# Retention and token-mixing kernel: full-height chunk tiles, decay on v and on the result, a new order of the steps

## The chip, the cores and the metric

The kernel runs on one core of one Trainium2 chip. The metric is the device time of one execution in microseconds (us). A profile covers the span from the first to the last instruction; the time is 1.7 to 2.0 us longer than the span (3.4 and 3.6 in two runs of experiment 11). Each run comes with the TensorE clock that was granted on average, and with a state: "slow" is put on a run that is over 1.5% above the fastest run of the same kernel.

In the profile PE is the matmul engine, PEld its weight loads, DVE the vector engine, ACT the scalar engine, POOL the GpSimd engine and SP the engine that issues most DMAs.

## The reference, cut to what matters

```python
# q, k, v: (4 batches, 8 heads, 768 tokens, 64); gamma[h] = 1 - 2**(-5-h)
for t in range(S):                         # retention, per batch and head
    state = gamma * state + outer(k[t], v[t])
    y[t]  = q[t] @ state / 8
x = y laid out as (batch, token, 512)      # then the token mixer
wq, wk = x @ w_q, x @ w_k                  # 512 x 64 each
mixed  = (wq @ wk.T / 8) @ x               # per batch; done as wq @ (wk.T @ x)
out    = relu(mixed) @ w_out               # 512 x 512
```

## The kernel before

The sequence is cut into 12 pairs of two 128-token chunks, three pairs per batch. The decay is folded into the operands: gamma^t times q and gamma^-t times k make the recurrence a plain masked product within a chunk (`sc`, `eat`, `ia`) plus a running state (`state`, `inter`). A load puts two consecutive tokens on each partition, so a chunk fills only 64 partitions, and everything whose contraction runs over tokens or over one head's 64 channels uses 64-row matmuls.

```python
def decay(e, p, name, table, half):              # q and k: cast and decay in one, 128 x 1024
    ENGINES[e].tensor_tensor(out=st[name + "s"]..., in0=st[name + "_st"]..., in1=table..., op=ALU.mult)
def cv(e, b, p):                                 # v: a plain cast, 128 x 1024
    copy(e, st["vs"]..., st["v_st"]...)
...
def sc(e, b, p, half):                           # scores: 16 matmuls of 64 x 64
    for hi in range(2):
        for j in range(2):
            for x in range(2):
                for c in range(2):
                    nc.tensor.matmul(out=ps[rows(c), x, hi, j, :], lhsT=st["kT"][rows(x), hp, j, c, :],
                                     rhs=st["qT"][rows(x), hp, c, :], ...)
...
def X(e, b, p):                                  # inter and state streams taken two and two in turn
    together(inter(p, 0), state(p, 1))
...
def ia(e, b, p, half):                           # masked scores times v: 16 matmuls, 64 rows each
    ... nc.tensor.matmul(out=st["y_ps"][:, c, x, hp, :], lhsT=st["at", half][rows(c), x, hi, j, :],
                         rhs=st["vs"][rows(c), hp, j, x, :], ...)
def ex(e, b, p):                                 # result out of PSUM: a plain cast
    copy(e, st["x"]..., st["y_ps"]...)
```

The order of all steps, with the engine of each evacuation and the PSUM bank, is a fixed list of tokens. `ex.3:A` is step `ex` of pair 3 on ACT (V is DVE, P is POOL), `sc.3.1@4` is the second half of the scores of pair 3 into bank 4. `trk` and `trq` transpose k and q, `xt` the result, `pj` is the projection by w_out, `eo` its evacuation, `fill` are matmuls on zeros that keep the array busy.

## Time and profile before

| | before |
|---|---|
| median of 3 runs | 106.53 us (106.33 to 107.72) |
| profiled run | 107.5 us, span 105.8, clock 0.96, state slow |
| last matmul group starts / last store lands | 94.09 / 105.8 us |
| loads | 20.19 MB, DMA full until about 70 us |

The prediction shows the slices, the stretches and the costly groups. Three lines of the page that it doesn't show matter later: the busy sums, ACT's slices (tenths of busy time, 40 slices of 2.65 us), and the queue that brings the instructions themselves (packets, MB, share of the DMA engines' time).

```profile
PE 90.7 (86%) x2040; PEld 63.3 (60%) x2040; DVE 77.0 (73%) x108; ACT 54.6 (52%) x87; POOL 46.1 (44%) x41
ACT  5103344713257546297679498648457184564010
...
q8 instruction: 16, 0.26, 1.0%
```

PE runs 2040 matmuls, and ACT and POOL are half idle: there is room there to pay for less PE work. The instruction queue moved 16 packets of 16 KB.

### The profile page before, as it was taken

Reading aid. Unit: us, or ns where it says so; the run is one execution under the profiler, and the core shown is the slowest. Engines: PE = TensorE matmul, PEld = TensorE weight load, DVE = VectorE, ACT = ScalarE, POOL = GpSimd, SP = SyncE. Lnnn points to the kernel's source line nnn. Section 1 sums busy time; section 2 is a strip of 40 time slices with the busy share of each in tenths; the row PEclk is TensorE's granted clock in tenths of the full one; section 3 lists DMA queues with packets and bytes.
Section 4 is the critical chain, followed back from the end, with each engine's and each line's share of the span. In section 5 each row is a group of like instructions: output and inputs, shape, how many; then the busy total and the mean of one; then the engine's idle time right before and its main releaser. Section 6 shows DMA issues by size and latency. Waiting matters only on the chain. (4 is left out here: it accounts for less than half of the span.)

```text
span 105.8 us, 4560 instructions
## 1 busy us (share of the span) xinstructions
PE 90.7 (86%) x2040; PEld 63.3 (60%) x2040; DVE 77.0 (73%) x108; ACT 54.6 (52%) x87; POOL 46.1 (44%) x41
## 2 busy tenths in 40 slices
PE   5997986849999996998999699689999999999800
PEld 2354664638888873595777566369668676554300
DVE  2097978836669899997589996999787976319800
ACT  5103344713257546297679498648457184564010
POOL 6620762985999315692977094990000000000000
PEclk9999999975599999999999999999999999999996
DMA  1999998999999999999999999999133060661993
GB/s 31 311 347 336 346 344 274 345 344 266 323 305 333 299 306 339 315 313 309 257 282 324 270 265 331 327 344 295 34 96 109 0 184 20 198 178 27 336 346 114
DMA packets 52324, 26.77 MB, mean 253 GB/s; under 512 B 848, under 2 KB 52304, under 8 KB 52304
## 3 DMA queue, kind: packets, MB, share of 16 engines
q1 hardware_dynamic: 51776, 26.22, 83.8%
q8 instruction: 16, 0.26, 1.0%
q10 hardware_dynamic: 528, 0.26, 0.8%
q14 instruction: 4, 0.03, 0.1%
HBM read 20.19 MB, written 6.29 MB: 250 GB/s over the span
## 5 line engine op out<-in xcount | busy, mean ns | idle before, releaser
L345 DVE TENSOR_TENSOR at_sb<-banks,cmask 128x1024 bf16<-128x1024 f32 x24 | 28.9, 1220 | 7.6 <-PE banks L333 7.4
L263 POOL TENSOR_TENSOR ks<-k_st,fk 128x1024 bf16<-128x1024 f32 (+1 forms) x10 | 18.4, 1841 | 13.7 <-DMA k_st<-in_k_dram 6.5
L569 PE MATMUL banks<-wout_sb,relu 128*128 128x512 bf16 x96 | 23.0, 379 | 1.2 <-DVE wout_sb L127 1.0
L263 POOL TENSOR_TENSOR qs<-q_st,fq 128x1024 bf16<-128x1024 f32 x9 | 17.6, 1956 | 6.9 <-DMA q_st<-in_q_dram 5.6
L126 ACT CAST x_nat<-banks 128x1024 bf16<-128x1024 f32 x11 | 11.1, 1012 | 8.2 <-PE banks L399 7.4
L569 PEld LDWEIGHTS <-relu 128*128 128x128 bf16 x96 | 8.6, 97 | 10.3 <-issue 1.7
L126 ACT COPY o_st<-banks 128x512 f32<-128x512 f32 x15 | 8.6, 589 | 9.0 <-PE banks L569 8.9
L333 PE MATMUL banks<-qT,kT 64*64 64x128 bf16 x384 | 10.6, 226 | 3.0 <-issue 1.6
L251 PE MATMUL banks<-warm 128*128 128x512 bf16 x32 | 10.2, 454 | 2.0 <-DVE warm L190 1.2
L333 PEld LDWEIGHTS <-kT 64*64 64x64 bf16 x384 | 7.0, 109 | 5.7 <-issue 2.4
L399 PE MATMUL banks<-s_sb,qT 64*64 64x64 bf16 x320 | 10.1, 200 | 0.1
L399 PE MATMUL banks<-vs,ks 64*64 64x64 bf16 x320 | 8.8, 194 | 1.3 <-issue 1.1
L436 PE MATMUL banks<-vs,at_sb 64*128 64x64 bf16 x384 | 9.3, 195 | 0.2 <-DVE at_sb L345 0.2
L562 ACT ACTIVATE relu<-banks 128x1024 bf16<-128x1024 f32 x7 | 7.2, 1027 | 4.0 <-PE banks L547 3.7
L477 PE MATMUL banks<-wqk_w,xT 128*128 128x128 bf16 x96 | 8.2, 234 | 1.1 <-issue 1.0
L126 ACT COPY kT<-banks 128x1024 bf16<-128x1024 bf16 x7 | 7.1, 1013 | 3.5 <-PE banks L297 3.2
L399 PEld LDWEIGHTS <-qT 64*64 64x64 bf16 x320 | 7.6, 112 | 2.0 <-issue 0.8
L463 PE MATMUL banks<-identity,x_nat 128*128 128x128 bf16 x96 | 8.1, 227 | 0.6 <-issue 0.5
L436 PEld LDWEIGHTS <-at_sb 64*128 64x128 bf16 x384 | 7.4, 97 | 2.0 <-issue 0.8
L477 PEld LDWEIGHTS <-xT 128*128 128x128 bf16 x96 | 6.5, 105 | 2.8 <-issue 1.3
L399 PEld LDWEIGHTS <-ks 64*64 64x64 bf16 x320 | 6.9, 109 | 1.8 <-issue 1.6
L126 ACT CAST s_sb<-banks 128x256 bf16<-128x256 f32 x14 | 5.3, 378 | 5.0 <-PE banks L399 5.0
(55 smaller groups left out, 135.5 us busy)
## 6 DMA issues: line engine op xcount, KB each, us to landing
q_st<-in_q_dram SPq DMA_DIRECT2D x12, 512.0 KB, 6.3
v_st<-in_v_dram SPq DMA_DIRECT2D x12, 512.0 KB, 6.7
k_st<-in_k_dram SPq DMA_DIRECT2D x11, 512.0 KB, 6.8
out_dram<-o_st SPq DMA_DIRECT2D x11, 512.0 KB, 4.3
wout_stage<-in_moe_w_out_dram SPq DMA_DIRECT2D x1, 1024.0 KB, 8.6
out_dram<-o_st SPq DMA_DIRECT2D x2, 256.0 KB, 3.3
k_st<-in_k_dram ACTq DMA_DIRECT2D x1, 256.0 KB, 4.3
k_st<-in_k_dram SPq DMA_DIRECT2D x1, 256.0 KB, 3.9
```

The lines of the kernel that those rows point to most:

```text
L126: return nc.scalar.copy(out=out, in_=in_)
L251: nc.tensor.matmul(out=bank32(b), lhsT=warm[:, 0:128], rhs=warm, start=True, stop=True)
L263: ENGINES[e].tensor_tensor(out=st[name + "s"][:, :, :, xs].rearrange("p hp j x d -> p x (hp j) d"), in0=st[name + "_st"][:, xs].rearrange( ...
L333: nc.tensor.matmul(out=ps[rows(c), x, hi, j, :], lhsT=st["kT"][rows(x), hp, j, c, :], rhs=st["qT"][rows(x), hp, c, :], start=(hi == 0 and ...
L345: ENGINES[e].tensor_tensor(out=st["at", half].rearrange("p x hi j t -> p (x hi) (j t)"), in0=st["at_ps", half].rearrange("p (xhi jt) -> p ...
L399: out.append(nc.tensor.matmul(skip_group_check=True, **mm))
L436: nc.tensor.matmul(out=st["y_ps"][:, c, x, hp, :], lhsT=st["at", half][rows(c), x, hi, j, :], rhs=st["vs"][rows(c), hp, j, x, :], start=fi ...
L463: nc.tensor.transpose(ps[:, a, c, :], st["x"][:, c, a, :], identity)
L477: nc.tensor.matmul(out=ps[:, c, :], lhsT=st["xT"][:, a, c, :], rhs=wqk_sb[:, a, :], start=(c == 0 and a == 0), stop=(a == NDM - 1), skip_g ...
L562: nc.scalar.activation(out=dst, in_=st["mx_ps"], func=ACT.Relu)
L569: nc.tensor.matmul(out=bank32(b), lhsT=st["relu"][:, a, j, :], rhs=wout_sb[:, a, :], start=(a == 0), stop=(a == NDM - 1),)
```

## The change

The intent: full-height (128-row) matmuls where there were pairs of half-height ones. For that the casts of k and v write the two tokens of a partition onto two different partitions, so that a chunk covers all 128. The scores and `inter` still contract over one head's 64 channels; they now fill all 128 output columns instead. Such a cast needs two instructions of 64 partitions x 512 elements per chunk. The decay moves from q and k to v (gamma^-t, table `fv`) and to the result (gamma^t, table `fy`), which makes q's cast a plain copy and the evacuation `ex` a multiply. Casts and evacuations are dealt out anew among the engines, and the whole order is new.

```diff
+    def ck(e, b, p, c):
+        for j in range(2):
+            copy(e, st["ks"][rows(j), c].rearrange("p hp x d -> p x hp d"),
+                    st["k_st"][rows(c), :, :, j])
+    def cv(e, b, p, c):
+        for j in range(2):
+            ENGINES[e].tensor_tensor(out=st["vs"][rows(j), c]..., in0=st["v_st"][rows(c), :, :, j],
+                                     in1=fv[rows(c), p % NP, :, j]..., op=ALU.mult)
...
     def sc(e, b, p, half):
-            for j in range(2):
+            for c in range(2):
                 for x in range(2):
-                    for c in range(2):
-                        nc.tensor.matmul(out=ps[rows(c), x, hi, j, :], lhsT=st["kT"][rows(x), hp, j, c, :], ...
+                    nc.tensor.matmul(out=ps[:, x, hi, c, :], lhsT=st["kT"][rows(x), hp, c, :], ...
...
-                        lhsT=st["ks"][rows(c), hp, j, x, :],     # state: 64 rows
-                        rhs=st["vs"][rows(c), hp, j, x, :],
+                    lhsT=st["ks"][:, c, hp, x, :],               # state: 128 rows
+                    rhs=st["vs"][:, c, hp, x, :],
...
-                            lhsT=st["at", half][rows(c), x, hi, j, :],   # ia
-                            rhs=st["vs"][rows(c), hp, j, x, :],
+                        lhsT=st["at", half][:, x, hi, c, :],
+                        rhs=st["vs"][:, c, hp, x, :],
...
     def ex(e, b, p):
-        copy(e, st["x"]..., st["y_ps"]...)
+        nc.vector.tensor_tensor(out=st["x"]..., in0=st["y_ps"]..., in1=fy[...].to_broadcast([128, 2 * H, D]), op=ALU.mult)
```

Left out here: the tables; the smaller mask; the two interleaved streams with their manual dependency, which become separate steps `st` and `in`; w_q and w_k loaded later and in 256-byte rows, w_out in four DMAs; the new order (W cast on ACT, WO on POOL, five more fills).

## The prediction

> **What bounds the kernel now.** I read first the slices of the page (busy tenths of each engine in 40 slices of 2.65 us, then the granted clock, the DMA share and the GB/s).
>
> ```profile
> PE   5997986849999996998999699689999999999800
> DVE  2097978836669899997589996999787976319800
> POOL 6620762985999315692977094990000000000000
> PEclk9999999975599999999999999999999999999996
> DMA  1999998999999999999999999999133060661993
> ```
>
> Two phases show. Until slice 28 (about 72 us) the DMA is full: it brings in q, k and v, and POOL, which casts them, ends with it. After that the DMA is mostly idle and PE alone is full until 100 us. The table of stretches (busy us of each engine in each stretch, clock, DMA share, GB/s) puts numbers to this:
>
> ```profile
> 6.00:30.00 24.00, 20.03 (x481) 15.30 (x481) 17.54 (x24) 9.12 (x11) 14.17 (x10) 0.86 1.08 322
> 30.00:70.00 40.00, 36.03 (x1023) 26.91 (x1015) 35.16 (x43) 26.47 (x43) 26.60 (x16) 1.00 1.05 307
> 70.00:90.00 20.00, 19.66 (x480) 14.48 (x470) 16.67 (x24) 12.22 (x23) 1.22 (x2) 1.00 0.41 122
> 90.00:100.30 10.30, 10.23 (x69) 4.86 (x68) 6.17 (x9) 4.58 (x8) 0.00 (x0) 1.00 0.61 183
> ```
>
> The columns are PE, weight load, DVE, ACT, POOL. From 30 to 70 us PE (90%) and DVE (88%) share the bound with loads at 307 GB/s; from 70 to 100.3 PE is 98% busy and nothing else is. The chain that ended last agrees: from 69.1 us on it is PE work with hardly a wait, and it ends so:
>
> ```profile
> 93.24 0.84 PE banks L547 x12
> 94.09 6.16 PE banks L569 x28
> 100.25 0.02 issue
> 100.27 0.58 ACT o_st L126
> ```
>
> Then 5 us of store follow to 105.8. POOL's timeline has the last v cast where the loads end, with no wait for DMA before it, so the last load had landed by 70.2:
>
> ```profile
> 70.19 1.03 POOL L127 CAST vs<-v_st 128x1024 bf16<-128x1024 f32 x1
> ```
>
> So 30 us of PE work are left when the last data is in. The end is set by how much PE work that is, and by when the last cast lets it start. The measured time is 1.7 us over the span (107.5 against 105.8 in the profiled run, a slow one; the median is 106.53).
>
> [...]in the chain eight transposes (N=128) take 0.45 us, 56 ns each, and four N=512 projections 0.86 us. [...]32 matmuls of 64x64 tiles took 0.38 us, 12 ns each. [...]the trace has 1.9 us and 1.04 us for 1024 elements[...]. [...]the trace's copy of 64x256 took 394 ns, the cast of 128x256 401. [...]the trace has the 1024-element v cast on DVE at 0.69 us beside an idle POOL and 2.38 us beside a busy one.
>
> **The change part by part.** I used these rows (count, busy us and mean ns):
>
> ```profile
> L345 DVE TENSOR_TENSOR at_sb<-banks,cmask 128x1024 bf16<-128x1024 f32 x24 | 28.9, 1220 | 7.6 <-PE banks L333 7.4
> L263 POOL TENSOR_TENSOR ks<-k_st,fk 128x512 bf16<-128x512 f32 x1 | 1.0, 1042 | 0.8 <-DMA k_st<-in_k_dram 0.8
> L126 ACT CAST x_nat<-banks 128x1024 bf16<-128x1024 f32 x11 | 11.1, 1012 | 8.2 <-PE banks L399 7.4
> L126 ACT COPY o_st<-banks 128x512 f32<-128x512 f32 x15 | 8.6, 589 | 9.0 <-PE banks L569 8.9
> L127 DVE COPY qT<-banks 128x1024 bf16<-128x1024 bf16 x9 | 6.2, 686 | 0.5 <-PE banks L312 0.5
> ```
>
> PE falls from 2040 matmuls to 1341. Scores: 16 to 8 per half, 0.23 to 0.42 us before in the chain (call it 0.32), 8x128 columns on two row tiles after, 0.22; 24 times, saves 2.4. State and inter: interleaved 0.38 us per 32 before, that is 0.25 alone and 0.38 together, 8.7 us by the old order's list; after, 20+20 groups of 8, 0.11 each, 4.4; saves 4.3. Result matmuls (ia): 16 to 8 per half, 0.285 to 0.22 (8 x 64 columns; it could be 0.285 again if the 128-column weight load holds them, since 36 ns per row tile is all that the trace shows for it); 24 times, saves 1.6. Five more warm-up matmuls cost 1.1. The sum of my list goes from 80.3 to 72.2 us, so **PE loses about 8 us**; 5 if the weight load holds ia and inter.
>
> The casts get dearer. Each 128-token chunk takes two half-height instructions of 512 elements, so a pair of chunks needs 4 x 512 per tensor where 1 x 1024 did. POOL: 22 v parts of two multiplies (2 x 1.0), 11 k parts of two casts (2 x 0.52), two q casts (1.04), the w_out cast (2.1): 44 + 11.4 + 2.1 + 2.1 = 60, with set-up 64, from 46. ACT: 13 k parts (2 x 0.6) 15.5, ten q casts (1.05) about 10; it loses x_nat (11.1) and v casts (3.2), and takes relu (7 to 10), o_st (15 to 17) and both weight casts: by my list 56.7 to 75.0. DVE: loses its k, q, v and w_out work from SBUF (14.4[...]), gains 12 result multiplies from PSUM at the rate of at_sb, 12 x 1.22 = 14.6, for one x_nat of 1.2; with fewer relus and o_st the list goes 81.0 to 76.5. These sums are of durations; back-to-back instructions start about 0.08 us (DVE) or 0.1 us (ACT) before the last has ended, so true occupancy is some 7 and 10 us less.
>
> DMA: bytes are the same, w_q and w_k are cut in 256-byte rows; under 1 us. The loads should still end near 68 to 70.
>
> **The path to the end.** POOL walks with the loads, and each pair (5.07 us at 310 GB/s) now gives it 3.7 us of v, 0.95 of k, and a little q: 4.9 us, 97% of the load pace, where it had 3.8. In the new order it does cv.10 and cv.11 last: four parts, 8 us. If it starts them when q11 is cast (about 68 us), the last ends at **76** rather than 71. By the order, 56 to 57 us of PE's list stand before the matmul that needs it (ia.11.1); at the old pace of 52 list-us by 69 us (0.75), PE is there at 75. DVE needs 63 and ACT 64 list-us by then, 0.9 and 0.92 of the time since 6 us, less the overlap: near full, but possible. After ia.11.1 PE has 15.6 list-us. The old tail ran 28 list-us in 31 us, so 17: PE ends at 93. The last evacuation and store took 5.5 us; the new order evacuates half of pair 9 last of all, which puts one copy (0.6) and a 512 KB store there: 6. Span 99, plus 1.7: 100.7. I take **100.5 us**.
>
> **Rivals.** (a) POOL keeps pace or isn't needed so late, and the loads' end (70 us) is the limit: ia.11.1 at 72, time 96.5. For it: POOL sat idle 6.5 us for k data and 5.6 for q data before, so it has room; against it: 44 multiplies at 1.0 us. (b) ACT or DVE becomes the bound: both need about 0.9 of the time, and the old DVE, the fullest of the three, had 0.88 in its best long stretch. If both fall to 0.82, ia.11.1 comes at 82 and the time is 106, the same as before. (c) The casts across partitions cost more than same-partition ones, or ACT's small instructions lose their overlap: 26 x 0.1 = 2.6 us on ACT, adding 1 to 2 us. (d) The throttle: 0.66 clock from 20 to 30 us cost nothing at the end before since loads went on, so a similar dip matters only if it falls after 70 us, then up to 3 us.
>
> **Range and chances.** (a) sets the low end, 96.5, and half of (b) the high end, 105.5. Faster by over 2% means under 104.4: 0.82. Within 2%: 0.13. Slower: 0.05.
>
> **What would show it.** Right: PE busy about 8 us less with 1341 matmuls; POOL near 64 us and busy until 74 to 77, its multiplies of 64x512 at 1.0 us; ACT about 70; about 17 us of PE after POOL's last cast, against 30. Wrong: POOL's half-height multiplies at 0.55 us (then a); PE with many waits on DVE or ACT between 30 and 75 us (b); ks copies on ACT over 0.7 us (c); ia at 36 ns per matmul (PE saves 5).

Of the rates that it gives ahead of "The change part by part", 1.9 and 1.04 us are POOL's multiply and cast of 128x1024 in the profile of before; the 394 and 401 ns are POOL's too, and that half the partitions would save nothing was inferred from these two. The matmul costs after the change are estimates, from the 56 ns of a 128-column transpose; no run measured a half-height matmul alone against one beside a partner.

## The result, and the profile after

The changed kernel took 103.31 us (median of 4 runs, 102.54 to 104.10), the kernel before 106.43 (4 runs, 106.17 to 107.72). The ratio is 0.966, with a 95% interval of 0.956 to 0.975. A ratio here is the mean time of one kernel's fast runs over that of the other's of the same rounds, so it isn't quite the ratio of the medians (0.971). The result is correct. The profiled run took 102.54 us, with a span of 100.6, a clock of 0.986.

The page after (busy sums, slices of 2.52 us, instruction queue):

```profile
PE 87.2 (87%) x1341; PEld 59.8 (59%) x1341; DVE 72.9 (72%) x108; ACT 71.8 (71%) x125; POOL 67.6 (67%) x86
...
PE   4995996999788997999998989999999999999300
...
ACT  4174879688987996989899999859947624645400
POOL 6541979999999999999999999999997000000000
PEclk9999999999999999999999999999999999999995
...
q8 instruction: 10, 0.16, 0.7%
```

POOL, which had gaps before, is now full from slice 5 to slice 31, and ACT nearly so. The granted clock has no dip. A third of the matmuls is gone, but only 3.5 us of PE's busy time: busy time counts overlapping matmuls once (before, 32 of `state` and `inter`, recorded at 0.19 to 0.22 us each, fill 0.38 us). The stretches (PE, weight load, DVE, ACT, POOL, then clock, DMA share, GB/s):

```profile
30.00:70.00 40.00, 37.63 (x680) 28.32 (x680) 34.69 (x44) 35.98 (x64) 37.54 (x42) 1.00 1.05 310
70.00:90.00 20.00, 19.92 (x280) 13.04 (x277) 15.64 (x21) 11.62 (x25) 7.12 (x7) 1.00 0.54 164
```

Between 30 and 70 us four engines are at 87 to 94%: PE and POOL 94, ACT 90, DVE 87. Before, only PE and DVE were near that (90 and 88). The costly new groups (count, busy us and mean ns, idle time before them):

```profile
L307 POOL TENSOR_TENSOR vs<-v_st,fv 64x512 bf16<-64x512 f32 x44 | 45.9, 1044 | 2.9
L134 POOL CAST ks<-k_st 64x512 bf16<-64x512 f32 x22 | 14.7, 667 | 5.7 <-DMA k_st<-in_k_dram 4.8
L133 ACT CAST ks<-k_st 64x512 bf16<-64x512 f32 x26 | 16.0, 615 | 2.9 <-DMA k_st<-in_k_dram 2.6
L458 DVE TENSOR_TENSOR x_nat<-banks,fy 128x1024 bf16<-128x1024 f32 x12 | 14.7, 1221 | 2.3 <-PE banks L444 2.1
```

POOL's timeline has the last v parts (start, duration), and the chain that ended last closes with the last projections:

```profile
68.69 8.83 POOL L307 TENSOR_TENSOR vs<-v_st,fv 64x512 bf16<-64x512 f32 x8
```

```profile
87.02 0.78 PE banks L556 x12
87.80 6.24 PE banks L578 x28
```

POOL ends at 77.5 us; the first matmul that needs its last part (`ia.11.1`) starts at 77.7. The page's chain of work that ended last lies on POOL for 33% of the span (25% on L307) and on PE for 28%, so by the profile alone POOL would be the gate. PE ends at 94.04 (it was 100.25), and the span at 100.6 (it was 105.8). So PE gained 6.2 us from profile to profile and the tail of stores gave 1.0 back. The profile of before is of a slow run and this one of a fast run, so part of the 6.2 us is the state.

### The profile page after: what moved, and what is told of

Same layout as the page of the kernel before. It is cut to its first block, busy times and chain, and to the rows that moved or that the text cites.

```text
span 100.6 us, 3245 instructions
## 1 busy us (share of the span) xinstructions
PE 87.2 (87%) x1341; PEld 59.8 (59%) x1341; DVE 72.9 (72%) x108; ACT 71.8 (71%) x125; POOL 67.6 (67%) x86
## 4 chain that ended last, share of the span: by engine, by line
POOL 33%; PE 28%; SPq 11%; issue 8%; DMA 7%; ACT 4%; POOLq 1%
POOL vs L307 25%; PE banks L578 13%; SPq L152 11%; DMA k_st<-in_k_dram 7%; POOL ks L134 7%; PE banks L444 2%; POOL qs L134 2%; PE banks L474 2%; PE banks L488 2%; PE banks L556 2%; PE banks L536 2%; PE banks L370 1%; PE banks L424 1%; ACT ks L133 1%; POOLq L655 1%
## 5 line engine op out<-in xcount | busy, mean ns | idle before, releaser
L307 POOL TENSOR_TENSOR vs<-v_st,fv 64x512 bf16<-64x512 f32 x44 | 45.9, 1044 | 2.9
L134 POOL CAST ks<-k_st 64x512 bf16<-64x512 f32 x22 | 14.7, 667 | 5.7 <-DMA k_st<-in_k_dram 4.8
L133 ACT CAST ks<-k_st 64x512 bf16<-64x512 f32 x26 | 16.0, 615 | 2.9 <-DMA k_st<-in_k_dram 2.6
L458 DVE TENSOR_TENSOR x_nat<-banks,fy 128x1024 bf16<-128x1024 f32 x12 | 14.7, 1221 | 2.3 <-PE banks L444 2.1
L133 ACT CAST qs<-q_st 128x1024 bf16<-128x1024 f32 (+1 forms) x10 | 10.1, 1006 | 0.4 <-DMA q_st<-in_q_dram 0.3
L444 PE MATMUL banks<-vs,at_sb 128*128 128x64 bf16 x192 | 8.8, 193 | 0.3 <-POOL vs L307 0.3
L370 PE MATMUL banks<-qT,kT 64*128 64x128 bf16 x192 | 8.3, 217 | 0.6 <-DVE wqn L134 0.2
L350 PE MATMUL banks<-identity,qs 128*128 128x128 bf16 x96 | 7.3, 219 | 0.8 <-ACT qs L133 0.5
L444 PEld LDWEIGHTS <-at_sb 128*128 128x128 bf16 x192 | 7.2, 98 | 1.3 <-issue 0.6
L424 PE MATMUL banks<-vs,ks 128*64 128x64 bf16 x160 | 6.3, 200 | 1.5 <-POOL vs L307 1.4
```

The lines of the kernel that those rows point to most:

```text
L133: return nc.scalar.copy(out=out, in_=in_)
L134: return ENGINES[e].tensor_copy(out=out, in_=in_)
L307: ENGINES[e].tensor_tensor(out=st["vs"][rows(j), c].rearrange("p hp x d -> p x hp d"), in0=st["v_st"][rows(c), :, :, j], in1=fv[rows(c), p ...
L370: nc.tensor.matmul(out=ps[:, x, hi, c, :], lhsT=st["kT"][rows(x), hp, c, :], rhs=st["qT"][rows(x), hp, c, :], start=(hi == 0 and c == 0), ...
L444: nc.tensor.matmul(out=y[:, x, c, hp, :], lhsT=st["at", half][:, x, hi, c, :], rhs=st["vs"][:, c, hp, x, :], start=first(p, x), stop=False ...
L458: nc.vector.tensor_tensor(out=st["x"].rearrange("p x c i n -> p (x c i n)").rearrange("p (m d) -> p m d", d=D), in0=st["y_ps"].rearrange(" ...
```

## The experiments

Twelve runs were made, in four batches, each batch on one chip beside fresh runs of the kernel before. Two theories stood at the start. **P**: POOL's last v multiply opens the end, as the prediction has it. **Q**: PE gets to that point at the same time by itself, because it and other engines are about equally full.

I use one derived figure below: the time from the first transpose of k of pair 6 (`trk.6`) to the first matmul of `ia.11.1`. Both are found by counting matmuls in the trace, and it covers the crowded part: 35.2 us in the changed kernel (42.5 to 77.7), and 35.2 and 35.7 in its profiles of experiments 1 and 12.

**1. The changed kernel again (first batch).** No edit.

> The changed kernel once more, as the yardstick of this batch. 102.5 to 104.1 us, 3 to 4% under the kernel before.

Median 102.25 us (101.94 to 104.09), mean of the fast runs 102.37, span 100.1, same profile. The kernel before took 102.77 to 110.0 on this chip (27 runs, median 106.34). Only 7 of the 27 were fast, with a mean of 103.5; against those the ratio is 0.989 (0.976 to 1.002). The medians differ by 3.8%. So the gain over the best runs of before is 1% and not clear of the noise, over its usual run almost 4%: the spread of the kernel before had to be explained too.

**2. POOL relieved.** POOL's v multiplies become plain casts (a wrong result).

```diff
+            if e == "P":
+                nc.gpsimd.tensor_copy(out=st["vs"][rows(j), c]..., in_=st["v_st"][rows(c), :, :, j])
+                continue
```

> POOL's 22 v parts become plain casts, without the decay (wrong result on purpose): two instructions of about 0.62 us each in place of 1.09, so POOL has some 20 us less work. Theory P (POOL's half-height multiplies pace the load phase and its last one, at 77.5 us, starts the last result matmul): the last v part is ready by about 72, and the time falls by 3 to 5 us, to about 99. Rival Q (PE itself, or ACT and DVE, would get to that matmul no earlier): under 1 us gained, 102.5 to 103.5.

```profile
PE 88.2 (87%) x1341; PEld 60.4 (60%) x1341; DVE 73.9 (73%) x108; ACT 71.5 (71%) x125; POOL 48.3 (48%) x86
...
L308 POOL CAST vs<-v_st 64x512 bf16<-64x512 f32 x44 | 27.2, 617 | 7.4 <-DMA v_st<-in_v_dram 4.3
```

The multiplies fell from 1044 to 617 ns and POOL lost 19 us of work; its last v part was ready at 74.7 us, nearly 3 us earlier (P had about 72; POOL now waited for loads). Yet `ia.11.1` started at 78.5 in the profiled run (a slow one, with a clock dip early on), and the stretch from `trk.6` took 35.3 us, the same as 35.2. The fast runs have a mean of 101.58, 0.8 us under the kernel of experiment 1. So P falls as a gate worth 3 to 5 us: without POOL's load PE came no earlier. POOL does release PE in the changed kernel, though. The trace has four waits of PE for v parts before 39 us, 1.7 us together, and the state group of the last v part but one starts 0.05 us after that part is done. But PE had waited only about 0.15 us there (it starts 0.46 us after the matmul before it; in experiments 2 and 4, where the part had long been ready, 0.31). The two arrive at nearly the same time, so taking one away gains little: 0.8 us in the means, with runs that overlap.

**3. The last stores in another order.** Half of pair 9 is evacuated by ACT ahead of the last relu, so that its 512 KB store doesn't come last.

```diff
-... pj.9.0@1 eo.6.1:A r.11:A pj.10.1@6 eo.10.1:A pj.10.0@2 pj.11.1@6 eo.9.0:V pj.11.0@1 eo.11.1:A eo.10.0:V eo.11.0:A eo.9.1:V
+... pj.9.0@1 eo.6.1:A eo.9.1:A r.11:A pj.10.1@6 eo.10.1:A pj.10.0@2 pj.11.1@6 eo.9.0:V pj.11.0@1 eo.10.0:V eo.11.1:A eo.11.0:A
```

> Only the last eight steps are put in another order: half of pair 9 is evacuated by ACT as soon as it is projected, pair 10's half before the last pair's, so the stores go out 9, 10, 11, 11 instead of 11, 10, 11, 9. If 1 us of the expected gain went into a worse store tail (6.5 us from the last PE result to the end, against 5.5 before), the time falls by 1 to 2 us, to about 101.8. If the DMA drain sets the tail whatever the order, under 0.4 us.

The issues of the stores at the end of the changed kernel, and of this version, against the last copy on ACT (start and duration):

```profile
94.06 0.59 ACT L133 COPY o_st<-banks 128x512 f32<-128x512 f32 x1 [0.28 <-PE banks L578]
94.27 0.45 SPq L609 DMA_DIRECT2D out_dram<-o_st  x1
94.82 0.68 SPq L611 DMA_DIRECT2D out_dram<-o_st  x1
95.59 0.67 SPq L609 DMA_DIRECT2D out_dram<-o_st  x1
```

```profile
92.97 0.37 SPq L609 DMA_DIRECT2D out_dram<-o_st  x1
93.15 0.58 ACT L133 COPY o_st<-banks 128x512 f32<-128x512 f32 x1 [1.11 <-PE banks L578]
93.76 1.24 SPq L611 DMA_DIRECT2D out_dram<-o_st  x2
94.01 0.58 ACT L133 COPY o_st<-banks 128x512 f32<-128x512 f32 x1 [0.28 <-PE banks L578]
```

L609 is the store of a whole pair (512 KB), L611 that of half a pair. The changed kernel issued two whole pairs after 94.2 us; here the last whole pair went out at 92.97. PE ended at the same time (94.0), and the span went from 100.1 to 98.3. Median 99.93 us (99.89 to 101.18), mean of the fast runs 100.15, 2.2% less than in experiment 1 and 0.968 (0.956 to 0.979) of before. The result is correct: this version beats both kernels.

**4. More PE work.** Twenty fills of 0.215 us (4.3 us together) are added ahead of transposes of pairs 4 to 10.

```diff
-... cq.4:A trk.4@3 ... ewq.0:A trq.4@1 ...
+... cq.4:A fill.1@3 trk.4@3 ... ewq.0:A fill.1@1 trq.4@1 ...      (20 such places)
```

> 20 idle warm-up matmuls of 0.215 us each (4.3 us of PE work) are spread over the transposes of pairs 4 to 10, all before POOL's last v part. Theory P (PE has slack in the load phase and waits for POOL): under 1.5 us lost. Rival Q (PE is as full as POOL there): 3 to 4.5 us lost, 106 to 107.5, which would also say that the PE work saved by full-height matmuls is worth its whole length in that phase.

Mean of the fast runs 103.85 (20 runs), 1.5 us above experiment 1: the very edge of P's forecast, and half of the least that Q had. About a third of the added PE time shows. If PE alone held the middle, all of it would; if another engine alone did, none. In this profile `ia.11.1` starts 1.5 us after POOL's last part (0.2 in the changed kernel), so here PE's own work held it. This speaks for a milder Q: PE shares the bound.

**5. The kernel before again (second batch).** No edit; another profile of it was wanted, for its clock.

> The kernel before, submitted as if it were a change, to get a second profile of it and its spread. In the first batch its 27 runs went from 102.8 to 110.0 us while the changed kernel's 6 went from 101.9 to 104.1. If the gaps without a releaser in the matmul stream (1.15 us at matmul 223 and 1.57 us at matmul 351, 128 matmuls or 16 KB of instructions apart) belong to the kernel and not to the chip, a fast profile has them shorter or without the clock dip that follows, and a slow one has them longer: spread 102.5 to 108, gaps again at multiples of 128 matmuls after 223. If the spread is the chip's, the gaps don't move with the time.

Median 106.07 us (102.73 to 107.28, 7 runs); the profiled run took 106.85, slow. This profile led to the likely cause of the spread. The first profile of before, PE's timeline, where the matmul stream stood still although the trace shows nothing that it waited for ("issue"):

```profile
16.85 0.21 PE L399 MATMUL banks<-vs,ks 64*64 64x64 bf16 x1 [1.15 <-issue]
...
22.50 0.42 PE L333 MATMUL banks<-qT,kT 64*64 64x128 bf16 x6 [1.57 <-issue]
...
49.59 0.23 PE L463 MATMUL banks<-identity,x_nat 128*128 128x128 bf16 x1 [0.49 <-issue]
...
59.80 0.23 PE L477 MATMUL banks<-wqk_w,xT 128*128 128x128 bf16 x1 [0.97 <-issue]
```

The stretches up to each of these count the matmuls before it (the second number in the PE column):

```profile
0.00:16.84 16.84, 13.35 (x223) 7.56 (x223) 10.86 (x23) 5.41 (x8) 7.95 (x17) 1.00 0.96 288
0.00:22.49 22.49, 17.29 (x351) 10.66 (x351) 14.22 (x26) 8.72 (x12) 12.08 (x21) 1.00 0.98 295
0.00:49.58 49.58, 42.72 (x991) 30.62 (x991) 36.87 (x55) 23.47 (x35) 30.48 (x32) 0.93 1.03 304
0.00:59.79 59.79, 51.95 (x1247) 37.84 (x1247) 45.25 (x65) 30.58 (x48) 37.12 (x36) 0.94 1.03 303
```

223, 351, 991 and 1247 all leave 95 when divided by 128. In this second profile the gaps stand at 223, 351, 863 and 1119 (1.15, 1.30, 1.53 and 1.20 us): again 95. A matmul comes with a weight load (the page counts 2040 of each), so 128 matmuls are 256 instructions. The instruction queue moved 16 packets of 16 KB for 2040 matmuls, and 2040 x 2 / 256 is 15.9: about one packet for every 256 instructions. So my reading, an inference from these counts, is **instruction fetch**: PE used up 256 instructions before the next 256 had come in, with the DMA share at 0.96 to 1.03 up to each gap of the first profile. The changed kernel has no such gap in its profile, nor have experiments 1 and 3.

The traces also hold the time of every DMA packet. They support the reading. In all fourteen profiles there are as many instruction packets as places 95, 223, 351 and so on in the stream (16 for 2040 matmuls, 10 for 1341, 12 for 1600). Each of the sixteen gaps, in the two profiles of before and in experiments 10 and 11, ends 1.2 to 1.6 us after the latest packet has landed, and no such place in any profile is passed sooner than that. In the changed kernel the packet had landed at least 2.8 us before each place.

At the end of the 1.57 us gap the granted clock fell to 0.5 for 6.8 us (the 7 and the two 5s in the slices that the prediction shows; it said that the dip cost nothing at the end), and in this second profile for 3.4 us right after the 1.30 us gap. A dip needs no such gap: in experiment 2 it came, for 3.4 us, after PE had waited 1.40 us for DVE, while waits for DVE of 1.50 us in experiment 12 and 1.98 us in experiment 11 were followed by none.

**6. All casts of k on POOL**, to relieve ACT (with the plain v casts of experiment 2, else POOL would be overfull; a wrong result).

```diff
     def ck(e, b, p, c):
+        e = "P"
```

> On top of the run with plain v casts on POOL (still a wrong result on purpose), all 24 k parts go to POOL: ACT loses 13 parts, 16 us, POOL has them and is still about 66 us full. If ACT, 90% busy from 30 to 70 us, is what holds PE in the load phase, the time falls 2 to 4 us below the 101.6 of the plain-cast run; if PE's own order and latency hold it, it stays within 0.7 us of it.

104.11 us (103.38 to 104.46), which neither forecast has. The start was spoiled: PE waited 3.48 us for a k cast at 22 us, and the clock dipped at the end of that wait. But the stretch from `trk.6` to `ia.11.1` took 32.9 us instead of 35.2.

**7. In addition the result's evacuation on ACT** as a plain copy, to relieve DVE (a wrong result).

```diff
-        nc.vector.tensor_tensor(out=st["x"]..., in0=st["y_ps"]..., in1=fy..., op=ALU.mult)
+        nc.scalar.copy(out=st["x"]..., in_=st["y_ps"]...)
```

> On top of that, the result goes to x by a plain copy on ACT in place of the multiply on DVE (wrong result on purpose): DVE loses 12 x 1.22 = 14.7 us, ACT gets back 12.2. If DVE (87% busy from 30 to 70 us) is the holder, 2 to 4 us less than the run before it; if none of the three engines is, about the same, or slower by what ACT gains.

108.51 us (107.94 to 108.81), worse: PE waited on ACT for the result in three places, 1.9 us together, and 4.56 us for a k cast at 22 us. The order is tuned to `ex` on DVE, and a move of one step upset more than it freed. It says nothing about DVE's share: inconclusive.

**8. Many small fills in the changed kernel.** Each of its 37 fills becomes eight of 64 columns, by estimate the same array time (an eighth of a fill's 0.215 us each), with 259 more matmuls: does the count alone bring the gaps back?

```diff
-        for _ in range(n):
+        for _ in range(8 * n):
-            ... out=bank32(b), lhsT=warm[:, 0:128], rhs=warm
+            ... out=bank32(b)[:, 0:64], lhsT=warm[:, 0:128], rhs=warm[:, 0:64]
```

> The changed kernel with each of its 37 warm-up matmuls of 512 columns cut into 8 of 64 columns: the same array time (8 x 27 ns against 215 ns), but 259 more matmuls, 518 more instructions, 33 KB, two more pieces of 16 KB. If a dense PE instruction stream outruns its own fetch beside full DMA queues, gaps without a releaser of 0.5 us or more appear before 30 us and the time rises by 1 to 4 us with a wider spread, like the kernel before. If the number of instructions doesn't matter, 102 to 103 us as without.

103.47 us (103.27 to 104.14), and the trace has 1600 matmuls, 12 instruction packets and no gap. Against experiment 1 that is 1.2 us more, but on another chip, where experiment 1 wasn't repeated. So more instructions alone, mostly at the start, aren't enough.

**9. The casts of k on POOL from pair 5 on only (third batch)**, to have experiment 6 without its spoiled start (a wrong result).

```diff
     def ck(e, b, p, c):
+        if p >= 5:
+            e = "P"
```

> Plain v casts on POOL (wrong result on purpose), and the k parts move from ACT to POOL only from pair 5 on, so the start, which spoiled the earlier run of this kind (PE waited 3.5 us for a k part at 22 us), stays as it is. ACT loses 8 parts, about 10 us, all in the load phase. If ACT's fullness (36 of 40 us from 30 to 70) holds PE there: 98 to 100 us, 2 to 3.5 below the 101.6 of the run with plain casts. If PE's own chain of small groups holds it: within 0.7 us of 101.6.

104.35 us (103.53 to 105.64), again outside both forecasts. The start was whole, but PE waited 1.41 us for a cast of q on ACT at 35 us and 3.79 us for one of k on POOL at 42 us, and the clock dipped again. After that, `trk.6` to `ia.11.1` took 32.3 us, 2.9 less than in the changed kernel. With ACT at 62.4 us of work instead of 71.8 PE went faster there, as in experiment 6. Both are weaker than they look: PE had been held up just before, so loads and casts had time to get ahead of it. ACT as a co-bound is likely, not shown. No version kept POOL and ACT both relieved without a wait elsewhere.

**10. The kernel before with its matmuls shifted.** Eight of the twenty opening fills become 72 of 64 columns: 64 more matmuls ahead of everything else, by estimate 0.2 us more array time (at an eighth of a fill's 0.215 us each). If the gaps belong to places in the program they stay there, and their count grows by 64; if they belong to every 256th instruction, the count keeps its remainder and the place moves.

```diff
+        if n == 20:
+            n = 12
+            for _ in range(72):
+                nc.tensor.matmul(out=bank32(b)[:, 0:64], lhsT=warm[:, 0:128], rhs=warm[:, 0:64], ...)
```

> The kernel before, with 8 of its 20 opening warm-up matmuls (N=512) given as 72 of N=64: the array time rises by 0.2 us, the count by 64 matmuls, 128 instructions, half a piece of 16 KB. In three places of two profiles of the kernel before the gaps without a releaser fall at matmul counts of 95 plus a multiple of 128 (223, 351, 863, 991, 1119, 1247). If they come from fetching the instruction stream, they stay at such counts, and so move by 64 matmuls in the program: the first two leave the state and score groups of pairs 1 and 2. If they belong to what the program does there, they move to 287 and 415. Time: the same as before, 103 to 107 with a wide spread, or 1 to 2 us less if the gaps now fall where PE waits anyway.

PE's timeline and the stretches up to the first two gaps:

```profile
19.61 0.51 PE L318 MATMUL banks<-identity,qs 128*128 128x128 bf16 x6 [0.66 <-issue]
...
25.81 0.51 PE L469 MATMUL banks<-identity,x_nat 128*128 128x128 bf16 x6 [2.46 <-issue]
```

```profile
0.00:19.60 19.60, 16.51 (x351) 11.91 (x351) 13.12 (x24) 7.61 (x11) 9.28 (x19) 1.00 0.94 279
0.00:25.80 25.80, 19.93 (x479) 14.58 (x479) 16.71 (x28) 9.00 (x13) 14.13 (x22) 1.00 0.98 288
```

351 and 479, and later 1247 and 1375: the remainder is 95 again, and the first two gaps now fall in transposes of q and of the result. The largest, 2.46 us, was followed by 3.4 us at half clock. 107.23 us (105.09 to 108.49). The edit shows that the gaps belong to counts of 95 plus a multiple of 128 matmuls, 256 instructions apart with the weight loads, and not to places in the program; that they are fetches is inferred from the packets, the latest of which landed 1.2 to 1.6 us before each gap ended (experiment 5).

**11. The changed kernel with 544 more matmuls (fourth batch).** Scores, `inter` and `ia` are cut into two 64-column tiles each, which I took to cost the same array time.

```diff
-                    nc.tensor.matmul(out=ps[:, x, hi, c, :], lhsT=st["kT"][rows(x), hp, c, :], ...
+                    for u in range(2):
+                        nc.tensor.matmul(out=ps[rows(u), x, hi, c, :],
+                                         lhsT=st["kT"][rows(x), hp, c, u * G : (u + 1) * G], ...
```

> The changed kernel with every score, inter and result matmul cut into two of 64 output columns of the array[...]: the same array time, the same casts and order, but 1885 matmuls instead of 1341 (2040 in the kernel before). Theory F (a good part of the gain is that PE's instruction stream is short enough for its fetch beside full DMA queues): gaps without a releaser come back at counts of 95 plus a multiple of 128, with clock dips, the time rises by 2 to 5 us to 104.5 to 107, and its spread grows to 3 us or more. Rival A (only array time and the order count): within 0.8 us of the changed kernel, no gaps.

106.42 us (105.38 to 108.22), mean of the fast runs 105.97. Gaps came back at remainder 95, four of them, 2.05 us together (counted in weight loads, since a few matmul records are missing). The largest:

```profile
67.32 0.35 PE L371 MATMUL banks<-qT,kT 64*64 64x128 bf16 x10 [0.83 <-issue]
```

No clock dip followed. But the premise failed. From the start of one group to the start of the next, a half of the scores took 0.35 us instead of mostly 0.33, one of `ia` 0.37 instead of 0.23 to 0.33, and over all groups that didn't wait the cut tiles took about 2.5 us more. So two causes are mixed in the 3.2 us that this kernel lost against the next one: denser instructions, and more array time. The spread that theory F forecast rests on the two slow runs, whose times lie 3.4 and 3.6 us above their spans.

**12. The changed kernel on the chip of experiment 11.** No edit.

> The changed kernel on the same chip as the run with half columns, as its yardstick: 102 to 103.5 us, spread under 2.5 us, no gap without a releaser in the matmul stream.

103.06 us (102.25 to 105.52), mean of the fast runs 102.79, no gap; 0.984 (0.976 to 0.991) of the fast runs of before on that chip, whose median was 106.31.

## Why the prediction was right or wrong

The forecast of 100.5 us with 96.5 to 105.5 held the result, and "faster" was right, for a partly wrong reason.

- **Less PE work**: half right. 1341 matmuls, and PE's tail after `ia.11.1` was 16.3 us where 17 was expected. But PE's busy time fell by 3.5 us (90.7 to 87.2; 90.3 in the other profile of before), not by the 8 that the prediction named as its sign. The costs after the change were set too low. By the trace's medians, from the start of one group to the start of the next, a state group took 0.25 us and an `inter` group 0.22 where 0.11 was expected; the scores took 0.33 for a half alone and 0.55 for two, where 0.22 each was expected. A half had taken 0.29 before, so the scores saved next to nothing. (The prediction's parts add up to 7.2, too, not to the 8.1 of its list.)
- **Dearer casts**: right. POOL 67.6 us (64 expected), its multiplies 1.044 us (1.0), starting 1.09 apart; ACT's casts of k 0.615 (0.6); DVE 72.9; ACT 71.8. The small miss was POOL's cast of k, 0.61 to 0.67 instead of 0.52.
- **The path to the end**: the time was nearly right, the gate was not. That POOL's end and PE's arrival, both later than forecast, fell together is luck. "If it starts them when q11 is cast (about 68 us), the last ends at 76": they started at 68.69 and ended at 77.5. But experiment 2 took this gate away and `ia.11.1` came no earlier. The step that failed is the sentence on PE: "at the old pace of 52 list-us by 69 us (0.75), PE is there at 75". It was there at 77.7 (77.2 to 78.5 in the profiles of experiments 1, 2, 3 and 12). That the PE work saved was less than forecast fits this, but no run isolates it. Between 30 and 70 us PE is 94% busy and a third of any added work shows (experiment 4): it is a co-bound of the middle, probably with ACT (experiments 6 and 9).
- **The tail**: 6.6 us after PE's end where 6 was expected, and 5.55 before. The cause was named rightly, and experiment 3 shows that it was avoidable: 2.2 us.
- **The sum**: 100.7 expected. PE ended 1.04 later (1.7 at `ia.11.1`, 0.7 won after it), the tail took 0.56 more, and the time lay 1.94 above the span instead of 1.7, 0.24 more. That makes 102.54, the profiled run; the median lies another 0.77 above it.
- **Rivals**: (a), that POOL isn't needed so late and the loads' end is the limit, fails in its time: with POOL relieved, `ia.11.1` didn't come at 72. (b), ACT or DVE near the bound, is partly true: ACT at 90% from 30 to 70 us. (c) doesn't hold on ACT (0.615 us). (d) didn't occur in the changed kernel.
- **What was missed altogether**: in the kernel before PE stood still four times with no releaser in the trace, 4.2 us together in one profile and 5.2 in the other (by experiment 5, probably for want of instructions), and a clock dip to 0.5 followed, 6.8 and 3.4 us long. I saw the dip and said that it "cost nothing at the end". The usual time of before, 106.5, contains this; its rarest runs (101.76 and 102.77 us, clock 0.999) are level with the changed kernel's. The dip isn't needed for a usual run: four runs of before at a clock of 0.997 to 0.998 took 106.6 to 107.1 us. Of the 60 runs of before that the four batches brought along, 43 took over 105 us; of 16 runs of the changed kernel (the first comparison and experiments 1 and 12) one did.

Open: both profiles of before are of slow runs, so that its fast runs lack the gaps is not shown, only likely. The 3.4% stands against four usual runs of before (106.2 us and more); against its fastest runs on two other chips the ratios are 0.989 and 0.984. And how much of the gain is saved array work and how much is the end of the gaps can't be told apart here, since experiment 11 mixed the two. Up to PE's end the profiles differ by 3.5 us of PE's busy time and 2.7 us of its idle time, while the gaps alone were 4.2; but the busy time of before holds 6.8 us at half clock. Nor did a run keep the old matmuls in the new order, so what the order alone gave is not known. Both profiles of before had reached `trk.9` by 60 us, as the changed kernel had (60.6), so the 6.2 us show only after that, where before has no gap left. Work held up earlier lies in that later part, though, so this doesn't settle it.

## What to carry to other kernels

When several engines are near 90% at the same place, the one that happens to finish last need not be the gate: take its load away before you believe it, and expect a fraction of any saving (here about a third of what was added to PE showed). Look at gaps on PE that nothing explains, and divide the number of matmuls before them: a constant remainder modulo 128 (95 here, at sixteen gaps) went with instruction packets that had landed only 1.2 to 1.6 us before the gaps ended. Fewer, larger matmuls may then pay beyond their array time, which these runs could not separate. At the end of a kernel, send the big stores first and the small ones last: that was 2.2 us for two lines of order.

## What the traces measured of the hardware

- At sixteen places of four profiles TensorE stood still for 0.15 to 2.46 us, each time after 95 plus a multiple of 128 matmuls, in a dense stream beside full DMA queues (before, 1023 matmuls from 30 to 70 us, at a DMA share of 1.05). The profile shows no such standstill with 680 matmuls in the same stretch after, at the same DMA share.
- Gaps of 1.30, 1.57 and 2.46 us and a wait of 1.40 us came with 3.4, 6.8, 3.4 and 3.4 us at half clock; gaps of 1.15, 1.20 and 1.53 us and waits of 1.50 and 1.98 us did not. So the clock fell with some of these stretches and not with longer ones, and no run shows what decides.
- 32 matmuls of 64x64 tiles took 0.38 us in the kernel before, 12 ns each, as the prediction says.
- In experiment 11, where each matmul of scores, `inter` and `ia` was cut into two 64-column tiles, they took about 2.5 us more in all for 544 more matmuls; a group of `ia` took 0.37 us instead of 0.23 to 0.33.
- On POOL half the partitions saved nothing in the multiply: one of 64x512 took 1044 ns after, one of 128x512 took 1042 before.
